# Block-sparse attention followed by a gated feed-forward layer: casting weight loads, g in the norm product, output projection between gate and value products, sums beside AV

## Chip, core and metric

One core of a Trainium2 chip. The metric is the device time of one execution in microseconds (us). Most executions of a kernel lie within 1%; a run counts as slow when it is more than 1.5% above the fastest of its kernel, and comparisons use the others. The profile is one traced execution. Its span is about 2 us shorter than the device time of the same execution, and "time from the start" below means time from the start of that span.

PE is TensorE (matmuls), PEld its weight loads, DVE VectorE, ACT ScalarE, POOL GpSimd, SP the queue that issues plain DMAs.

## The reference

```python
# q, k, v: [4, 8, 768, 64] float32; blocks of 32 tokens, 3 sampled blocks a row of blocks
scores = q @ k.T / 8
mask = |block_i - block_j| <= 1, or either is the first or last block, or block_j is sampled
attn = softmax(where(mask, scores, -1e9))
x = (attn @ v) as [3072, 512]                    # heads side by side
xn = x / sqrt(mean(x*x) + 1e-6) * rms_g
y = (silu(xn @ w_gate) * (xn @ w_val)) @ w_out   # 512 -> 1536 -> 512, float32 out
```

## The kernel before

The work is cut into 8 units of 384 query tokens (2 a batch). Each unit has 4 pairs of heads, and each pair 6 steps. In a step PE makes two score products (128 keys by 384 queries, one for each head) into one of two score tiles (`ps_s`, two PSUM banks each), and ACT takes the exponential of both. Beside it run the attention output (AV), the row sums, the norm, and the feed-forward products of the unit before. The instruction order on every engine is the order in which the program emits it. So the emission order is the schedule, and an instruction that has to wait holds up all that stand behind it on its engine.

The parts that matter here (cuts are marked `# ...`):

```python
# PSUM: 8 banks. ps_s 2 x 2 banks (scores, transposes, norm); ps_a acc, zw; ps_f gp, vp
def load_w_chunk(i):                       # at steps 5, 9, 13, 17
    for w, src, mul in ((wg, wgv, 1.0), (wv, wvv, 0.5)):
        st = wst.tile([P, DM // P, FCH], FP32, name="wstage", tag="wstage")
        # ...
        nc.sync.dma_start(out=st, in_=src[:, :, f0:f0 + FCH])
        for c in range(DM // P):
            nc.vector.tensor_scalar(out=w[:, c, f0:f0 + FCH], in0=st[:, c, :],
                scalar1=gcol[:, c:c + 1], scalar2=mul, op0=ALU.mult, op1=ALU.mult)

def transposes(b, pr):                     # q and k of one pair of heads, 24 products
    t_ = ps_s.tile([P, 2, 1024], BF16, name="tqk", tag="s")
    # ...
    nc.vector.tensor_copy(out=QTe[0:D, sl, :], in_=t_[0:D, 0, 0:S])
    nc.scalar.copy(out=KTe[0:D, sl, :], in_=t_[0:D, 1, 0:S])
    nc.vector.tensor_copy(out=QTo[D:P, sl, :], in_=t_[D:P, 0, 0:S])
    nc.scalar.copy(out=KTo[D:P, sl, :], in_=t_[D:P, 1, 0:S])

def ff_g(u, f):                            # gate: 4 products, tanh on ACT, uu on DVE
    if u == NU - 1:                        # last unit: gate and value in one score tile
        gv = ps_s.tile([P, 2, 512], FP32, name="gv", tag="s"); gp = gv[:, 0, 0:TG]
    else:
        gv = None; gp = ps_f.tile([P, TG], FP32, name="gp", tag="gp")
    # 4 matmuls; th = tanh(gp / 2); uu = (th + 1) * gp

# the schedule: fixed items at a step, feed-forward items by a credit
at(s1 + 1, av, n); at(s1 + 2, zsum, n); at(s1 + 4, wsum, n)
if pr == NP - 1:
    at(s1 + 4, norm_a, u); at(s1 + 5, norm_b, u); at(s1 + 6, norm_c, u)
    at(s1 + 7, norm_d, u, 0); at(s1 + 7, norm_d, u, 1)
# ...
for u in range(NU):
    for f in range(NF):
        items.append((0.64, ff_g, (u, f))); items.append((0.64, ff_v, (u, f)))
    for t in range(NT):                    # output projection after all of them
        for part in range(2):
            items.append((1.3, ff_y, (u, t, part, 2)))
```

The softmax here doesn't subtract the row's maximum and nothing guards it: scores larger than these inputs give would overflow.

Of the kernel before, what the change touches and what calls it, by code (L numbers as in the profile page):

```python
# [17 lines left out]
def kernel(  # L18
# [13 lines left out]
    P = 128  # L32
# [17 lines left out]
    raw = ctx.enter_context(tc.tile_pool(name="raw", bufs=3))  # L50
# [4 lines left out]
    wst = ctx.enter_context(tc.tile_pool(name="wst", bufs=2))  # L55
# [10 lines left out]
    def load_qk(b, pr):  # L66
        qb = raw.tile([P, 2, NC * D], BF16, name="qb", tag="qb")
        kb = raw.tile([P, 2, NC * D], BF16, name="kb", tag="kb")
        nc.gpsimd.dma_start(out=qb, in_=qv[b, :, 2 * pr:2 * pr + 2, :])  # L69
        nc.gpsimd.dma_start(out=kb, in_=kv[b, :, 2 * pr:2 * pr + 2, :])  # L70
        return qb, kb

    vtiles = {}

    def load_v(b, lo, hi):
        if b not in vtiles:
            vtiles[b] = vpool.tile([P, H, NC * D], BF16, name="vb", tag="vb")
        nc.gpsimd.dma_start(out=vtiles[b][:, lo:hi, :], in_=vv[b, :, lo:hi, :])

    qk_raw = {(0, 0): load_qk(0, 0)}  # L80

    ident = const.tile([P, P], BF16, name="ident")
    make_identity(nc, ident)

    samp_i = const.tile([32, NRND], I32, name="samp_i")
# [3 lines left out]
    nc.sync.dma_start(out=samp_i[0:NB, :], in_=s64[:, 0:2 * NRND:2])  # L89
    gcol = const.tile([P, DM // P], FP32, name="gcol")  # L90
    nc.sync.dma_start(out=gcol, in_=moe_rms_g.rearrange("(c p) -> p c", p=P))


    Bm = const.tile([32, 32], BF16, name="Bm")
    nc.gpsimd.memset(Bm, 1.0)
# [11 lines left out]
    jb = const.tile([32, 32], I32, name="jb")  # L107
    nc.gpsimd.iota(jb, pattern=[[1, 32]], base=0, channel_multiplier=0)

    Kind = const.tile([32, NC, P], BF16, name="Kind")  # L110
    nc.gpsimd.memset(Kind, 1.0)
# [6 lines left out]
    Kindf = Kind.rearrange("b c p -> b (c p)")  # L118
    load_v(0, 0, 2)
    for pr in range(1, NP):  # L120
        if pr < 3:
            qk_raw[(0, pr)] = load_qk(0, pr)
        load_v(0, 2 * pr, 2 * pr + 2)
# [4 lines left out]
    nc.vector.tensor_copy(out=samp_f[0:NB, :], in_=samp_i[0:NB, :])  # L128
    onehot = const.tile([32, 32], BF16, name="onehot")
    for r in range(NRND):  # L130
        nc.vector.tensor_scalar(
            out=onehot[0:NB, 0:NB], in0=jbf[0:NB, 0:NB],
            scalar1=samp_f[0:NB, r:r + 1], scalar2=None, op0=ALU.is_equal)
        nc.vector.tensor_tensor(
            out=Bm[0:NB, 0:NB], in0=Bm[0:NB, 0:NB], in1=onehot[0:NB, 0:NB], op=ALU.max)
# [3 lines left out]



    KTe = const.tile([P, NSLOT, S], BF16, name="KTe")
    KTo = const.tile([P, NSLOT, S], BF16, name="KTo")
    QTe = const.tile([P, NSLOT, S], BF16, name="QTe")
    QTo = const.tile([P, NSLOT, S], BF16, name="QTo")
    Qmask = const.tile([32, S], BF16, name="Qmask")
    qm = ps_s.tile([P, 2, 512], FP32, name="qm", tag="s")
    for ic in range(2):
# [3 lines left out]
    nc.vector.tensor_copy(  # L152
        out=Qmask.rearrange("b (i t) -> b i t", i=2), in_=qm[0:32, :, 0:TG])

    def mask_rows(sl):
        for row, KT, QT in ((64, KTe, QTe), (0, KTo, QTo), (32, KTo, QTo)):
            nc.vector.tensor_copy(out=KT[row:row + 32, sl, :], in_=Kindf)
            nc.vector.tensor_copy(out=QT[row:row + 32, sl, :], in_=Qmask)
# [8 lines left out]
    Ew = const.tile([P, NP, 32], BF16, name="Ew")  # L167
    nc.gpsimd.memset(Ew, 0.0)
    for e in range(2):
        h0 = 64 * e  # L170
        nc.gpsimd.affine_select(
            out=Ew[h0:h0 + 64], in_=Ew[h0:h0 + 64], compare_op=ALU.not_equal, fill=1.0,
            base=16 + e, pattern=[[2, NP], [-1, 32]], channel_multiplier=0)
# [3 lines left out]
    for half in range(2):  # L177
# [5 lines left out]
        base=-16, pattern=[[-1, 8]], channel_multiplier=1)  # L183
# [12 lines left out]

    wg = const.tile([P, DM // P, DFF], BF16, name="wg")
    wv = const.tile([P, DM // P, DFF], BF16, name="wv")
    wo = const.tile([P, NF, DM], BF16, name="wo")

    FCH = 384
    wgv = moe_w_gate.rearrange("(c p) f -> p c f", p=P)
    wvv = moe_w_val.rearrange("(c p) f -> p c f", p=P)

    def load_w_chunk(i):
        f0 = i * FCH
        for w, src, mul in ((wg, wgv, 1.0), (wv, wvv, 0.5)):
            st = wst.tile([P, DM // P, FCH], FP32, name="wstage", tag="wstage")
            if i == 0:
                nc.vector.memset(st[0:1, 0, 0:1], 0.0)  # L210
            nc.sync.dma_start(out=st, in_=src[:, :, f0:f0 + FCH])
            for c in range(DM // P):
                nc.vector.tensor_scalar(
                    out=w[:, c, f0:f0 + FCH], in0=st[:, c, :], scalar1=gcol[:, c:c + 1],
                    scalar2=mul, op0=ALU.mult, op1=ALU.mult)

    def load_wo():
        nc.gpsimd.dma_start(out=wo, in_=moe_w_out.rearrange("(c p) f -> p c f", p=P))

    def transposes(b, pr):  # L220
        sl = (b * NP + pr) % NSLOT
        qb, kb = qk_raw.pop((b, pr))
        t_ = ps_s.tile([P, 2, 1024], BF16, name="tqk", tag="s")
        for e, src in enumerate((qb, kb)):
            for c in range(NC):
                for h in range(2):
                    nc.tensor.transpose(  # L227
                        out=t_[64 * h:64 * h + 64, e, c * P:(c + 1) * P],
                        in_=src[:, h, c * D:(c + 1) * D], identity=ident)
        nc.vector.tensor_copy(out=QTe[0:D, sl, :], in_=t_[0:D, 0, 0:S])  # L230
        nc.scalar.copy(out=KTe[0:D, sl, :], in_=t_[0:D, 1, 0:S])  # L231
        nc.vector.tensor_copy(out=QTo[D:P, sl, :], in_=t_[D:P, 0, 0:S])  # L232
        nc.scalar.copy(out=KTo[D:P, sl, :], in_=t_[D:P, 1, 0:S])  # L233
# [3 lines left out]
    def qk_exp(n, jt):  # L237
        u, pr = divmod(n, NP)
        b, ic = divmod(u, 2)
        sl = (b * NP + pr) % NSLOT  # L240
        if jt == 0:
            ptiles[n] = ppool.tile([P, NC, 2, TG], BF16, name="pt", tag="pt")
        s_ = ps_s.tile([P, 2, 512], FP32, name="s_", tag="s")
        for e, (KT, QT, K) in enumerate(((KTe, QTe, 64 + NB), (KTo, QTo, P))):
            nc.tensor.matmul(  # L245
                out=s_[:, e, 0:TG],
                lhsT=KT[0:K, sl, jt * P:(jt + 1) * P],
                rhs=QT[0:K, sl, ic * TG:(ic + 1) * TG], start=True, stop=True)
        nc.scalar.activation(  # L249
            out=ptiles[n][:, jt, :, :], in_=s_[:, :, 0:TG], func=AF.Exp, scale=SCALE)  # L250

    def av(n):
# [3 lines left out]
        if pr == 0:  # L256
            osb[u] = opool.tile([P, NP, TG], FP32, name="osb", tag="osb")
            zwt[u] = ps_a.tile([P, 512], FP32, name="zw", tag="zw")[:, 0:TG]
        o_ = ps_a.tile([P, 512], FP32, name="o_", tag="acc")
        for jt in range(NC):  # L260
            for e in range(2):
                nc.tensor.matmul(  # L262
                    out=o_[64 * e:64 * e + 64, 0:TG],
# [3 lines left out]
        nc.scalar.copy(out=osb[u][:, pr, :], in_=o_[:, 0:TG])  # L267
        o2 = work.tile([P, TG], BF16, name="o2", tag="o2")
        nc.gpsimd.tensor_tensor(
            out=o2, in0=osb[u][:, pr, :], in1=osb[u][:, pr, :], op=ALU.mult)  # L270
        o2s[n] = o2
# [13 lines left out]
    def wsum(n):  # L285
        u, pr = divmod(n, NP)
        nc.tensor.matmul(
            out=zwt[u][0:32, :], lhsT=Ew[:, pr, :], rhs=o2s.pop(n),
            start=False, stop=(pr == NP - 1), skip_group_check=True)

    nrm = {}

    def norm_a(u):
        zs = work.tile([P, TG], FP32, name="zs", tag="zs")
        nc.vector.tensor_copy(out=zs, in_=zwt.pop(u))
        nrm[u] = zs

    def norm_b(u):
        zs = nrm[u]
        zt = ps_s.tile([P, NT, 16], FP32, name="zt", tag="s")  # L300
        for t in range(NT):
            nc.tensor.matmul(
                out=zt[:, t, :], lhsT=zs[:, t * P:(t + 1) * P], rhs=Sel,
                start=True, stop=True)
        rz = work.tile([P, NT, 8], FP32, name="rz", tag="rz")
        nc.vector.reciprocal(out=rz, in_=zt[:, :, 0:8])
        w1 = work.tile([P, NT, 8], FP32, name="w1", tag="w1")
        nc.vector.tensor_tensor(out=w1, in0=zt[:, :, 8:16], in1=rz, op=ALU.mult)
# [6 lines left out]
        nc.gpsimd.tensor_tensor(out=rs, in0=ms, in1=nhalf, op=ALU.pow)  # L315
        fx = work.tile([P, NT, 8], FP32, name="fx", tag="fx")
# [7 lines left out]
    def norm_c(u):  # L324
# [10 lines left out]
    def norm_d(u, half):  # L335
# [4 lines left out]
        for i in range(2):  # L340
# [4 lines left out]
        nc.vector.tensor_tensor(  # L345
            out=xns[u][:, 2 * half:2 * half + 2, :],
            in0=osb[u][:, 2 * half:2 * half + 2, :], in1=fb[:, :, 0:TG], op=ALU.mult)
# [3 lines left out]
    def ff_g(u, f):  # L351
        if f == 0:
            hps[u] = ffw.tile([P, NF, TG], BF16, name="hp", tag="hp", bufs=2)
        if u == NU - 1:
            gv = ps_s.tile([P, 2, 512], FP32, name="gv", tag="s")
            gp = gv[:, 0, 0:TG]
        else:
            gv = None
            gp = ps_f.tile([P, TG], FP32, name="gp", tag="gp")
# [9 lines left out]
        gst[(u, f)] = (uu, gv)  # L369

    def ff_v(u, f):
# [133 lines left out]
```

## Time and profile before

The median is 485.74 us (485.72 to 487.21, 3 runs). The profiled execution took 489.61 us, with a span of 487.7 us.

| stretch of the profiled run | us |
|---|---|
| first exponential starts | 16.5 |
| 36th exponential starts (end of "the opening") | 87.3 |
| 36th to last exponential | 337.8 |
| last exponential to the end | 62.6 |
| 24 steps (one unit) in the middle, mean of five | 53.2 |
| PE idle before an instruction, after the 36th exponential, summed | 57.8 |

From the page: busy time of the engines, then the span in 40 slices. A digit is a busy share in tenths (9 is 90% or more). PEclk is the granted PE clock in tenths of full speed.

```profile
span 487.7 us, 6743 instructions
...
PE 385.8 (79%) x2730; PEld 189.7 (39%) x2730; DVE 185.6 (38%) x392; ACT 251.4 (52%) x385; POOL 73.0 (15%) x112
...
PE   1554387988788978998788989997889989987556
...
PEclk9985787999899999999899999999998999998999
```

PE is busiest, but its row has low digits at the start (up to the seventh slice) and at the end, and 7s in between. The PEclk row has many digits below 9. (Its first two digits say little: the record of the granted clock begins with its first change, 27.2 us from the start, and the score products before that last 0.51 us, as they do at half clock, against 0.33 us at full clock.)

The opening, from the timeline (start, duration, engine, line, operation, then in brackets the idle time of that engine just before it and what ended it):

```profile
29.40 0.50 PE L227 MATMUL tqk<-ident,kb 128*64 128x128 bf16 x12
...
36.95 1.41 DVE L213 TENSOR_SCALAR wv<-wstage,gcol 128x384 bf16<-128x384 f32 x4 [6.15 <-DMA wstage<-in_moe_w_val_dram]
...
40.30 0.55 DVE L230 COPY QTe<-tqk 64x768 bf16<-64x768 bf16 x1
...
42.30 0.79 ACT L233 COPY KTo<-tqk 64x768 bf16<-64x768 bf16 x1 [0.63 <-DVE QTo L232]
...
43.15 0.48 PE L245 MATMUL s__421<-QTe,KTe 88*128 88x384 bf16 x1 [12.38 <-ACT KTo L233]
```

The transposes of the third pair end at 29.9 us. Their first copy on DVE starts at 40.30 us, because DVE first stands at the weight scaling of `wv` until the staged load has landed (6.15 us of idle), and then makes six mask copies (38.39 to 40.27 us). The transposes hold one of the two score tiles until their last copy ends, on ACT at 43.1 us, and the exponential that would free the other stands behind that copy on ACT. So the next score product (`s__421`) waits 12.38 us on PE.

What PE waited for in the whole run, from the view of waits (who, for whom: us in total, times, longest):

```profile
PE gp L361 <- DVE uu L367: 18.9, 35, 2.0
PE gv L375 <- DVE uu L367: 14.0, 12, 1.2
PE s__421 L245 <- ACT KTo L233: 12.4, 1, 12.4
...
PE s__526 L245 <- ACT KTo L233: 7.2, 1, 7.2
PE ft L328 <- DVE FHL_192 L321: 6.7, 4, 2.5
PE ft L328 <- DVE FHL_193 L321: 4.0, 3, 1.5
```

The gate bank is single. One round of it in the timeline of all engines:

```profile
297.72 0.81 PE L361 MATMUL gp<-xn,wg 128*128 128x384 bf16 x4 [0.40 <-DVE uu L367]
...
298.57 0.49 ACT L365 ACTIVATE th<-gp 128x384 bf16<-128x384 f32 x1 [0.40 <-PE gp L361]
...
299.09 0.55 DVE L367 SCALAR_TENSOR_TENSOR uu<-th,gp 128x384 bf16<-128x384 bf16 x1 [0.76 <-ACT th L365]
...
299.70 0.81 PE L361 MATMUL gp<-xn,wg 128*128 128x384 bf16 x4 [0.18 <-DVE uu L367]
```

Gate product to next gate product is 1.98 us: product, tanh, uu, next product. The value products and a step's score products do not fill it, and PE waits 0.18 to 0.40 us here.

Last, the clock, from busy times by stretch (PE, PEld, DVE, ACT, POOL busy with counts, then granted clock, DMA share, GB/s):

```profile
350.00:351.00 1.00, 0.00 (x0) 0.00 (x0) 0.36 (x1) 1.00 (x3) 0.00 (x0) 1.00 0.00 0
...
352.00:353.00 1.00, 1.00 (x5) 0.47 (x4) 0.00 (x0) 0.35 (x1) 0.00 (x0) 0.50 0.00 0
```

After a gap of about 1.3 us and others just before it, the granted clock is 0.50 for 3.4 us. Adding up the record after the 36th exponential gives 20.5 us at half clock.

### The profile page before, as it was taken

The page shows a single profiled execution, that of the slowest core. Times are in us where ns is not written, and L with a number is a line of the kernel's source. Part 1 is how long each engine was busy: PE and PEld are TensorE (multiplying, and loading weights), DVE is VectorE, ACT ScalarE, POOL GpSimd, SP SyncE. Part 2 cuts the span into 40 slices and gives each one's busy share as a digit, 9 for nine tenths or more (in the row PEclk, how much of TensorE's full clock was granted, in tenths as well). Part 3 has the DMA queues.
Part 4 walks back from the last instruction along what each step waited for, and adds up shares of the span by engine and source line. Part 5 has one row for each costly group of instructions (what it writes and reads, how often), then busy time and mean ns, then how long its engine had stood idle before and what let it go on. Part 6 is the DMA issues. An engine that isn't in the chain of part 4 may idle for free.

```text
span 487.7 us, 6743 instructions
## 1 busy us (share of the span) xinstructions
PE 385.8 (79%) x2730; PEld 189.7 (39%) x2730; DVE 185.6 (38%) x392; ACT 251.4 (52%) x385; POOL 73.0 (15%) x112
## 2 busy tenths in 40 slices
PE   1554387988788978998788989997889989987556
PEld 1221133444344434544344434543344434433322
DVE  4416743542344412443244333434244224433440
ACT  1534474665466644675466646665556546612121
POOL 8710122011011011011111020010000010010000
PEclk9985787999899999999899999999998999998999
DMA  5976762311322013223032015021000000010001
GB/s 68 146 186 215 195 102 42 53 24 31 77 34 32 2 43 53 35 34 55 30 46 34 0 44 87 1 34 43 23 1 0 23 30 15 0 40 27 1 0 65
DMA packets 22786, 24.02 MB, mean 49 GB/s; under 512 B 1764, under 2 KB 19684, under 8 KB 22756
## 3 DMA queue, kind: packets, MB, share of 16 engines
q0 software_dynamic: 14464, 11.01, 16.2%
q1 hardware_dynamic: 8292, 12.59, 7.3%
q8 instruction: 21, 0.34, 0.3%
q14 instruction: 9, 0.07, 0.1%
HBM read 28.31 MB, written 6.29 MB: 71 GB/s over the span
## 4 chain that ended last, share of the span: by engine, by line
PE 57%; DVE 15%; ACT 15%; issue 5%; DMA 4%; POOL 2%; POOLq 0%; ACTq 0%; DVEq 0%
PE gp L361 11%; PE yp L389 11%; PE vp L375 7%; DVE uu L367 5%; ACT th L365 5%; PE zw L280 4%; ACT pt L249 3%; ACT KTe L231 3%; DMA wstage<-in_moe_w_val_dram 3%; PE tqk L227 2%; PE gv L375 2%; ACT KTo L233 2%; DVE QTo L232 2%; DVE QTe L230 2%; PE gv L361 2%
## 5 line engine op out<-in xcount | busy, mean ns | idle before, releaser
L367 DVE SCALAR_TENSOR_TENSOR uu<-th,gp 128x384 bf16<-128x384 bf16 x84 | 46.5, 554 | 104.0 <-ACT th L365 104.0
L361 PE MATMUL gp<-xn,wg 128*128 128x384 bf16 x336 | 70.0, 331 | 18.9 <-DVE uu L367 18.9
L389 PE MATMUL yp<-wo,hp 128*128 128x512 bf16 x288 | 73.7, 398 | 6.1 <-ACT yo L395 3.4
L375 PE MATMUL vp<-xn,wv 128*128 128x384 bf16 x336 | 69.9, 331 | 1.3 <-DVE hp L378 1.3
L365 ACT ACTIVATE th<-gp 128x384 bf16<-128x384 f32 x84 | 41.2, 490 | 35.9 <-PE gp L361 35.1
L378 DVE TENSOR_TENSOR hp<-uu,vp 128x384 bf16<-128x384 bf16 x84 | 46.6, 554 | 25.5 <-PE vp L375 19.0
L361 PEld LDWEIGHTS <-wg 128*128 128x128 bf16 x384 | 35.4, 98 | 53.4 <-issue 34.4
L375 PEld LDWEIGHTS <-wv 128*128 128x128 bf16 x384 | 35.6, 98 | 46.9 <-issue 26.5
L389 PEld LDWEIGHTS <-hp 128*128 128x128 bf16 x288 | 28.3, 103 | 39.5 <-issue 15.1
L245 PEld LDWEIGHTS <-KTo 128*128 128x128 bf16 x192 | 19.4, 101 | 42.8 <-issue 30.8
L395 ACT COPY yo<-yp 128x512 f32<-128x512 f32 x24 | 14.0, 585 | 34.5 <-PE yp L389 34.3
L231 ACT COPY KTe<-tqk 64x768 bf16<-64x768 bf16 x16 | 12.7, 792 | 36.2 <-DVE QTe L230 36.2
L245 PEld LDWEIGHTS <-KTe 88*128 88x128 bf16 x192 | 19.6, 102 | 26.3 <-issue 10.3
L262 PEld LDWEIGHTS <-vb 128*64 128x64 bf16 x384 | 21.0, 117 | 21.4 <-issue 13.7
L280 PE MATMUL zw<-pt,Ez 128*32 128x384 bf16 x384 | 22.2, 338 | 0.0
L230 DVE COPY QTe<-tqk 64x768 bf16<-64x768 bf16 x16 | 8.8, 550 | 33.2 <-PE tqk L227 33.0
L345 DVE TENSOR_TENSOR xn<-osb,fb 128x768 bf16<-128x768 f32 x16 | 14.8, 952 | 16.7 <-PE fb L342 16.6
L375 PE MATMUL gv<-xn,wv 128*128 128x384 bf16 x48 | 9.7, 324 | 14.0 <-DVE uu L367 14.0
L365 ACT ACTIVATE th<-gv 128x384 bf16<-128x384 f32 x12 | 5.9, 490 | 23.6 <-PE gv L361 23.5
L233 ACT COPY KTo<-tqk 64x768 bf16<-64x768 bf16 x16 | 12.7, 793 | 10.0 <-DVE QTo L232 10.0
L69 POOL DMA_DIRECT2D qb<-in_q_dram x16 | 12.3, 768 | 25.9 <-PE tqk L227 25.1
L315 POOL TENSOR_TENSOR rs<-ms,nhalf 128x3 f32<-128x3 f32 x8 | 7.0, 869 | 51.5 <-DVE ms L312 51.5
(800 smaller groups left out, 568.6 us busy)
## 6 DMA issues: line engine op xcount, KB each, us to landing
out_dram<-yo SPq DMA_DIRECT2D x24, 256.0 KB, 2.0
qb<-in_q_dram POOLq DMA_DIRECT2D x16, 192.0 KB, 3.8
kb<-in_k_dram POOLq DMA_DIRECT2D x16, 192.0 KB, 4.3
wstage<-in_moe_w_gate_dram SPq DMA_DIRECT2D x4, 768.0 KB, 6.4
wstage<-in_moe_w_val_dram SPq DMA_DIRECT2D x4, 768.0 KB, 5.9
vb<-in_v_dram POOLq DMA_DIRECT2D x3, 768.0 KB, 7.2
wo<-in_moe_w_out_dram POOLq DMA_DIRECT2D x1, 1536.0 KB, 11.9
vb<-in_v_dram POOLq DMA_DIRECT2D x4, 192.0 KB, 6.2
```

The lines of the kernel that those rows point to most:

```text
L230: nc.vector.tensor_copy(out=QTe[0:D, sl, :], in_=t_[0:D, 0, 0:S])
L231: nc.scalar.copy(out=KTe[0:D, sl, :], in_=t_[0:D, 1, 0:S])
L233: nc.scalar.copy(out=KTo[D:P, sl, :], in_=t_[D:P, 1, 0:S])
L245: nc.tensor.matmul(out=s_[:, e, 0:TG], lhsT=KT[0:K, sl, jt * P:(jt + 1) * P], rhs=QT[0:K, sl, ic * TG:(ic + 1) * TG], start=True, stop=True)
L262: nc.tensor.matmul(out=o_[64 * e:64 * e + 64, 0:TG], lhsT=vb[:, 2 * pr + e, jt * D:(jt + 1) * D], rhs=pt_[:, jt, e, :], start=(jt == 0), s ...
L280: nc.tensor.matmul(out=zwt[u][32 * c:32 * c + 32, :], lhsT=Ez[:, pr, :], rhs=pt_[:, 2 * j2 + par, e, :], start=(pr == 0 and j2 == 0), stop ...
L361: nc.tensor.matmul(out=gp, lhsT=wg[:, c, f * P:(f + 1) * P], rhs=xns[u][:, c, :], start=(c == 0), stop=(c == NP - 1))
L365: nc.scalar.activation(out=th, in_=gp, func=AF.Tanh, scale=0.5)
L367: nc.vector.scalar_tensor_tensor(out=uu, in0=th, scalar=1.0, in1=gp, op0=ALU.add, op1=ALU.mult)
L375: nc.tensor.matmul(out=vp, lhsT=wv[:, c, f * P:(f + 1) * P], rhs=xns[u][:, c, :], start=(c == 0), stop=(c == NP - 1))
L378: nc.vector.tensor_tensor(out=hps[u][:, f, :], in0=uu, in1=vp, op=ALU.mult)
L389: nc.tensor.matmul(out=yp, lhsT=hps[u][:, f, t * P:(t + 1) * P], rhs=wo[:, f, :], start=(f == 0), stop=(f == NF - 1))
```

## The change

The intent is to keep PE supplied throughout. The weights come in bf16 by casting loads, so DVE no longer scales them; g goes into the norm product and the factor 0.5 into the output copy. The output projection of the unit before is spread between the gate and value products of this one. The row sums come straight after AV, and the square sums of a unit come together at its end, as a set of four products in four column groups of PE, in place of four single products at four times. Further parts belong to it: transposes are evicted by two DVE copies in place of four alternating ones, osb and most output copies move from ACT to DVE, AV uses a score bank from pair 8 on, norm steps are spread over more steps, the last unit's gate and value products alternate between two kinds of bank, and q and k are loaded by whole batches.

```diff
-    def load_w_chunk(i):  ... staged float32 loads, 8 DVE scalings a chunk ...
+    def load_w(i):
+        nc.gpsimd.dma_start(out=wg[:, :, i * FH:(i + 1) * FH], in_=wgv[:, :, ...])
+        nc.gpsimd.dma_start(out=wv[:, :, i * FH:(i + 1) * FH], in_=wvv[:, :, ...])
@@ norm product @@
-        nc.vector.tensor_tensor(out=xns[u][:, 2 * half:2 * half + 2, :], in0=osb..., in1=fb..., op=ALU.mult)
+        for i in range(2):
+            nc.vector.scalar_tensor_tensor(out=xns[u][:, pr, :], in0=osb[u][:, pr, :],
+                scalar=gcol[:, pr:pr + 1], in1=fb[:, i, 0:TG], op0=ALU.mult, op1=ALU.mult)
@@ transposes @@
-        four copies QTe (DVE), KTe (ACT), QTo (DVE), KTo (ACT)
+        nc.vector.tensor_copy(out=XE[0:D, sl], in_=t_[0:D, :, 0:S])
+        nc.vector.tensor_copy(out=XO[D:P, sl], in_=t_[D:P, :, 0:S])
@@ mask rows: all slots before the first step @@
+    load_w(0); mask_rows(2); load_w(1); mask_rows(3); load_wo(); mask_rows(4); mask_rows(5)
@@ schedule @@
-        at(s1 + 1, av, n); at(s1 + 2, zsum, n); at(s1 + 4, wsum, n)
+        at(s1 + 1, 1.1, av, n, n >= 8); at(s1 + 1, 0.7, zsum, n)
-            norm_a .. norm_d at s1 + 4, + 5, + 6, + 7, + 7
+            norm_a .. norm_e at s1 + 4, + 5, + 7, + 8, + 9, + 10
@@ feed-forward queue @@
-    gate and value of unit u, then 6 projection parts of unit u
+    for f in range(NF):
+        ffq.append((avail, 0.65, ff_g, (u, f, wide)))
+        ffq.append((avail, 0.65, ff_v, (u, f, wide)))
+        ffq.append((avail, 0.65, ff_y, (u - 1, f // 4, f % 4, 4)))
```

(The loops that guard the first and last unit, and the set-up of constants, are left out.)

## The prediction

> **What bounds the kernel now.** The page gives PE 79% busy of a 487.7 us span, ACT 52%, DVE 38%: PE is the bound, but only in the middle. From the starts of exponentials and tanh in the timeline:
>
> - Opening: the 36th exponential starts at 87.3 us. DVE's in-order weight scaling waits for staged weights (6.6 and 6.2 us) ahead of the copies of the transposes: the score product waits 12.4 us, then 7.2 us (waits view, 22 to 60 us).
> - Middle: 52.4 us a unit of 24 steps. Start-to-start times of dense matmuls (0.162 us for 384 columns, 0.216 for 512, about 1.7 us for AV plus sums, 0.7 for a set of transposes) add up to some 43 us; 9 are idle: at the single gate bank (gate, tanh 0.49, uu 0.55, next gate: 1.98 us cycle), at the norm chain (1.5 us before ft, 8 times) and at the transposes' four serial copies (2.9 us, holding a score bank).
> - Tail: last exponential at 425.1 us, then 62.6 us. The last unit's gate/value pairs take 2.63 us each for 1.3 us of products; its output projection comes after.
>
> **What changes.**
> 1. Casting weight loads, g in the norm product: removes 32 scalings (11.9 us of DVE) and, more, their waits. The Trainium skill, "DMA: Bandwidth & Descriptors", section "SWDGE vs HWDGE vs iDMA", says a casting DMA must be issued from GpSimd; in this trace that queue moved 11.01 MB for 16.2% of 16 engines' span, some 139 GB/s flat out. By that estimate 7 MB of first inputs and weights needs about 51 us, in the order of need; no stall expected.
> 2. New cost: the mask copies of all other slots (20 x about 0.35 us) stand ahead of the second transposes' copies on DVE: a 6 to 9 us hole after the first three exponentials. First exponential at about 13 us instead of 16.5, 36th at about 60 instead of 87: 27 us won.
> 3. Output projection between gate and value: successive gate products lie about 2.3 us of PE work apart, over the 1.98 us cycle. Norm steps are spread. Transposes: two DVE copies of about 1 us; they still hold a score bank, and I expect 1.9 us lost, 12 times, less than before.
> 4. ACT gives osb, most yo and KT copies to DVE; estimate 26 us a unit on each, neither bounding.
>
> **Sum.** From step 35 on, dense PE work is about 309 us; transposes' holds 23; first unit without projection 5; norms and rest 11; output 4. 60 + 352 = 412 us span, less 2 (span against time here): **410 us**, range 392 to 432. Faster by over 2%: 0.97; within 2%: 0.02; slower: 0.01.
>
> **What would show it.** Right: no PE wait for DMA at 30 to 60 us; the middle at about 46 us a unit; PE above 88% busy from 80 us on; tanh of the last unit about 2.0 us apart; the largest remaining PE wait is the score product behind DVE copies XE/XO. Wrong: gate products still waiting for uu; wo or wg awaited.
>
> **What would make it wrong.** The clock: the Trainium skill, "TensorE: Matmul & The Clock Gate", section "What's actually happening", says an idle window halves the PE clock until it has been busy for about 3.4 us. This trace agrees: after idle at 350 and 364 us the granted clock is 0.50. If 1.9 us holds trigger it, add up to 20 us; if not, the gain is larger, since before pays it. Other risks: GpSimd slowed by issuing weight loads, delaying mask rows; DVE queue order delaying uu.

## The result, and the profile after

The changed kernel takes 402.1 us median (399.99 to 406.36, 4 runs) against 486.48 us (485.72 to 488.08, 4 runs). The ratio is 0.8247, with a 95% interval of 0.8186 to 0.8309. Ratios are the mean time of one kernel's fast runs over that of the other's of the same rounds, so they are not quite the ratio of the medians. In these four runs the granted clock was 1.0 twice (399.99 and 400.38 us) and 0.977 to 0.979 twice (403.82 and 406.36 us, the latter counted as slow). The profiled executions are one of 489.61 us before and the fastest, of 399.99 us, after, so the differences of the stretches below add up to some 5 us more than those of the medians.

The same lines of the page:

```profile
span 398.3 us, 6628 instructions
...
PE 352.3 (88%) x2730; PEld 187.0 (47%) x2730; DVE 217.8 (55%) x423; ACT 200.4 (50%) x301; POOL 66.8 (17%) x95
...
PE   2657879887799999998999999998999999999986
...
PEclk9999999999999999999999999999999999999999
```

From the twelfth slice on PE is at 9 nearly everywhere, and the clock row has 9 throughout. For the first 27.3 us that 9 is no measurement: here too the record begins only then, and the score products before it last 0.51 us, against 0.33 us afterwards.

| stretch | before | after | difference |
|---|---|---|---|
| first exponential starts | 16.5 | 11.7 | -4.8 |
| 36th exponential starts | 87.3 | 59.0 | -28.3 |
| from there to the end | 400.3 | 339.3 | -61.0 |
| of that, PE idle before an instruction | 57.8 | 19.4 | -38.4 |
| of that, time at half clock | 20.5 | 0.0 | -20.5 |
| recorded time at half clock in the opening | 30.7 | 0.0 | -30.7 |
| one unit in the middle, mean of five | 53.2 | 42.9 | -10.3 |
| last exponential to the end | 62.6 | 58.9 | -3.7 |

(The last line holds more work than before: at the last exponential 9 of the 12 gate and value steps of the seventh unit are still to come.)

The waits of PE after the change, in the same view:

```profile
PE tqk L161 <- DMA qb<-in_q_dram: 5.1, 1, 5.1
...
PE ft L327 <- ACT pt L242: 2.7, 3, 0.9
...
PE gp L361 <- DVE uu L367: 2.4, 9, 0.5
...
PE s__283 L238 <- ACT pt L242: 0.9, 1, 0.9
```

The gate product's wait for uu has fallen from 18.9 to 2.4 us, and the last unit's (`gv`, 14.0 us) is gone. A round of the gate in the middle shows why:

```profile
240.17 0.81 PE L361 MATMUL gp<-xn,wg 128*128 128x384 bf16 x4
...
240.82 0.81 PE L378 MATMUL vp<-xn,wv 128*128 128x384 bf16 x4
241.07 0.48 ACT L365 ACTIVATE th<-gp 128x384 bf16<-128x384 f32 x1
...
241.59 0.55 DVE L367 SCALAR_TENSOR_TENSOR uu<-th,gp 128x384 bf16<-128x384 bf16 x1 [0.86 <-ACT th L365]
...
241.80 0.81 PE L392 MATMUL yp<-wo,hp 128*128 128x512 bf16 x3
...
242.44 0.81 PE L361 MATMUL gp<-xn,wg 128*128 128x384 bf16 x4
```

The chain of gate, tanh and uu ends at 242.14 us, but PE has value, score and projection products to do until 242.44 us. The next gate product starts with no wait. What is left is seen after each set of transposes (PE alone):

```profile
248.83 0.50 PE L161 MATMUL tqk<-ident,kb 128*64 128x128 bf16 x12
...
249.44 0.33 PE L238 MATMUL s__2944<-XO 128*128 128x384 bf16 x1
250.66 0.32 PE L238 MATMUL s__2948<-XE 88*128 88x384 bf16 x1 [0.90 <-ACT pt L242]
```

The product at 250.66 us waits 0.90 us for an exponential. Such a wait stands after each of the twelve sets of transposes in the rest, nine times before a score product and three times before `ft`. The transposes hold one score bank, so the next two steps share the other.

### The profile page after: what moved, and what is told of

The parts are those of the page before. It is cut to its first block, busy times and chain, and to the rows that moved or that the text cites. A ratio compares the mean times of both kernels' runs of the same rounds, so it can differ in the third digit from the quotient of the medians.

```text
span 398.3 us, 6628 instructions
## 1 busy us (share of the span) xinstructions
PE 352.3 (88%) x2730; PEld 187.0 (47%) x2730; DVE 217.8 (55%) x423; ACT 200.4 (50%) x301; POOL 66.8 (17%) x95
## 4 chain that ended last, share of the span: by engine, by line
PE 79%; ACT 9%; DVE 8%; issue 2%; DMA 1%; POOL 1%; DVEq 0%; POOLq 0%; ACTq 0%
PE gp L361 14%; PE yp L392 14%; PE vp L378 13%; ACT pt L242 6%; PE zw L275 5%; PE tqk L161 3%; PE oa L259 2%; DVE uu L367 2%; ACT th L365 1%; PE fb L341 1%; PE zt L295 1%; DVE xn L346 1%; DMA out_dram<-yo 1%; PE gw L361 1%; DVE XE L183 1%
## 5 line engine op out<-in xcount | busy, mean ns | idle before, releaser
L238 PEld LDWEIGHTS <-XO 128*128 128x128 bf16 x192 | 19.0, 99 | 40.7 <-issue 30.8
L238 PEld LDWEIGHTS <-XE 88*128 88x128 bf16 x192 | 19.1, 99 | 26.5 <-issue 6.7
L259 PEld LDWEIGHTS <-vb 128*64 128x64 bf16 x384 | 19.5, 111 | 17.7 <-issue 11.1
L346 DVE SCALAR_TENSOR_TENSOR xn<-osb,gcol,fb 128x384 bf16<-128x384 f32 x32 | 18.2, 610 | 9.0 <-PE fb L341 9.0
L164 DVE COPY XE<-tqk 64x1536 bf16<-64x1536 bf16 x16 | 15.2, 949 | 11.5 <-PE tqk L161 11.5
L165 DVE COPY XO<-tqk 64x1536 bf16<-64x1536 bf16 x16 | 15.4, 960 | 0.2
L401 DVE TENSOR_SCALAR yo<-yp 128x512 f32<-128x512 f32 x21 | 14.4, 685 | 1.2 <-PE yp L392 1.1
L161 PE MATMUL tqk<-ident,qb 128*64 128x128 bf16 x192 | 9.1, 234 | 5.3 <-DMA qb<-in_q_dram 5.1
L264 DVE COPY osb<-oa 128x384 f32<-128x384 f32 x8 | 4.5, 556 | 17.1 <-PE oa L259 17.1
L275 PEld LDWEIGHTS <-Ez 128*32 128x32 bf16 x384 | 7.3, 95 | 11.8 <-issue 10.1
L161 PEld LDWEIGHTS <-qb 128*64 128x64 bf16 x192 | 6.4, 116 | 10.4 <-issue 5.3
## 6 DMA issues: line engine op xcount, KB each, us to landing
kb<-in_k_dram POOLq DMA_DIRECT2D x3, 768.0 KB, 10.3
```

What stands on the lines that cost most here:

```text
L161: nc.tensor.transpose(out=t_[64 * h:64 * h + 64, e, c * P:(c + 1) * P], in_=src[:, 2 * pr + h, c * D:(c + 1) * D], identity=ident)
L238: nc.tensor.matmul(out=s_[:, e, 0:TG], lhsT=X[0:K, sl, 1, jt * P:(jt + 1) * P], rhs=X[0:K, sl, 0, ic * TG:(ic + 1) * TG], start=True, stop ...
L259: nc.tensor.matmul(out=o_[64 * e:64 * e + 64, :], lhsT=vb[:, 2 * pr + e, jt * D:(jt + 1) * D], rhs=pt_[:, jt, e, :], start=(jt == 0), stop ...
L275: nc.tensor.matmul(out=zwt[u][32 * c:32 * c + 32, :], lhsT=Ez[:, pr, :], rhs=pt_[:, 2 * j2 + par, e, :], start=(pr == 0 and j2 == 0), stop ...
L346: nc.vector.scalar_tensor_tensor(out=xns[u][:, pr, :], in0=osb[u][:, pr, :], scalar=gcol[:, pr:pr + 1], in1=fb[:, i, 0:TG], op0=ALU.mult, ...
```

## The experiments

All were correct within the tolerance. "Opening" is the start of the 36th exponential in the profiled run, "rest" is from there to the end of the span. The rest of the changed kernel was 339.3 us in both profiles of it. Its opening was 59.0 and 61.4 us.

| run | edit | median us | ratio to before | opening | rest | PE idle in the rest | half clock, opening / rest |
|---|---|---|---|---|---|---|---|
| before | | 488.17 to 489.43 | 1 | 87.3 | 400.3 | 57.8 | 30.7 / 20.5 |
| r_after | the change again | 404.18 | 0.8251 (0.8214 to 0.8288) | 61.4 | 339.3 | 21.0 | 3.4 / 0.0 |
| b1_cast | before + casting loads | 473.73 | 0.9692 (0.9663 to 0.9721) | 70.5 | 402.8 | 57.6 | 10.2 / 27.3 |
| e2_stage | change - casting loads | 418.14 | 0.8567 (0.8525 to 0.8610) | 77.2 | 339.2 | 19.4 | 30.7 / 0.0 |
| e1_seq | change - interleaving | 427.36 | 0.8756 (0.8709 to 0.8803) | 60.3 | 364.7 | 36.0 | 3.4 / 0.0 |
| e7_act | change, osb and yo on ACT | 402.47 | 0.8244 (0.8203 to 0.8285) | 60.8 | 340.5 | 19.0 | 13.7 / 3.4 |
| e6_sums | change - sums beside AV | 399.75 | 0.8179 (0.8155 to 0.8203) | 57.6 | 340.9 | 14.0 | 10.2 / 3.4 |
| e8_norm | change - spread norm | 427.55 | 0.8733 (0.8705 to 0.8760) | 64.2 | 361.7 | 37.0 | 10.2 / 13.7 |
| e9_copies | change, four alternating copies | 447.53 | 0.9157 (0.9131 to 0.9182) | 74.4 | 371.7 | 39.1 | 10.2 / 34.1 |
| e10_last | change, last unit in one tile | 421.22 | 0.8587 (0.8556 to 0.8618) | 63.0 | 356.3 | 34.6 | 6.8 / 3.4 |
| e3_masks | change + late mask copies | 399.64 | 0.8164 (0.8127 to 0.8201) | 55.8 | 340.8 | 21.0 | 3.4 / 3.4 |
| e4_fill | change + filled steps | 398.93 | 0.8163 (0.8129 to 0.8197) | 64.3 | 334.9 | 14.2 | 14.5 / 6.0 |
| e11_best | both + row sums a step later | 387.01 | 0.7914 (0.7892 to 0.7936) | 53.7 | 331.3 | 13.9 | 3.4 / 0.0 |

(The last column is us at half clock in the profiled run: in the opening as far as recorded, in the rest up to PE's last product.) b1, e1, e2 and e7 ran on one chip in one set; r_after, e3, e4 and e6 in a second; e8, e9, e10 and e11 in a third, each set with its own runs of before. The changed kernel itself was run again only in the second set, so across sets the ratios are compared, not the times.

The opening also differs where no edit touches it: e10_last changes only the last unit, and its opening was 63.0 us, against 59.0 and 61.4 us. The recorded half clock in it differs too (6.8, 0.0 and 3.4 us). So differences of a few us in the opening are not put down to an edit on their own.

The theory: two separate gains. In the opening, DVE no longer waits for staged weights ahead of the copies that PE needs. In the rest, PE is the bound, and the change closes its waits, above all that of the gate bank, by putting other products there. The rivals are named in each expectation.

### b1_cast: the kernel before with casting loads alone

```diff
-            nc.sync.dma_start(out=st, in_=src[:, :, f0:f0 + FCH])   # and 4 DVE scalings
+            nc.gpsimd.dma_start(out=w[:, :, f0:f0 + FCH], in_=src[:, :, f0:f0 + FCH])
@@ g in the norm product, yo = 0.5 * yp on ACT @@
```

> The kernel before with only the weight loads changed: casting loads on the GpSimd queue, g in the norm product, 0.5 in the output copy. Theory A (the opening was held by the weight scaling standing in DVE's order and waiting for the staged loads): the 36th exponential starts at about 62 to 70 us instead of 87.3, the 12.4 us and 7.2 us waits of the score product are gone, time 460 to 470 us. Rival B (the opening is held by the arrival of q, k, v or by score banks, and other parts of the change won it): 36th exponential after 80 us, time 478 us or more. Middle and tail as before, 52 us a unit, in both.

The time was 473.73 us. The 12.4 and 7.2 us waits were gone. The 36th exponential came at 70.5 us, 16.8 us earlier, just outside the span that I had given, and the time missed it by 4 us. So the weight staging is the largest part of the opening's 28.3 us, but not all of it. The rest did not gain (402.8 us; 27.3 us of it at half clock, against 20.5).

### e2_stage: the change with staged loads again

```diff
+            nc.sync.dma_start(out=st, in_=src[:, :, f0:f0 + FCH])   # fp32 stage, steps 5, 9, 13, 17
+            for c in range(DM // P):
+                nc.vector.tensor_copy(out=w[:, c, f0:f0 + FCH], in_=st[:, c, :])
```

> The changed kernel with the weights staged as float32 through the SP queue and copied to bf16 by DVE in the places of the old scaling (no g, so the result stays right). Theory A: DVE's copies wait for the staged loads ahead of the transposes' copies; the 36th exponential goes from 59 to 72 to 85 us and the time to 413 to 428 us. Rival B: 36th exponential before 64 us, time 406 us or less.

The time was 418.14 us, the 36th exponential came at 77.2 us, and the rest was 339.2 us, that of the changed kernel to a tenth. Taking the staging out of one kernel gave 16.8 us, and putting it into the other cost 15.8 to 18.2 us. Part of this may be the clock: with staging both openings have 30.7 us at recorded half clock, without it 10.2 (b1_cast) and 0.0 or 3.4 us (the changed kernel). What the waits alone would cost was not separated. Two waits of the score product behind DVE's copies were back, in the view of waits:

```profile
PE s__403 L243 <- DVE XE L171: 8.0, 1, 8.0
PE s__309 L243 <- DVE XE L171: 7.6, 1, 7.6
```

Rival B falls. What the weights do not explain of the opening (some 10 to 12 us) belongs to other parts: the first exponential is 4.8 us earlier (in b1_cast it is still at 16.5 us), and the remainder was not tried part by part.

### e1_seq: projection after the gate and value products

```diff
         for f in range(NF):
             ffq.append((avail, 0.65, ff_g, (u, f, wide)))
             ffq.append((avail, 0.65, ff_v, (u, f, wide)))
-            ffq.append((avail, 0.65, ff_y, (u - 1, f // 4, f % 4, 4)))
+        for f in range(NF):
+            ffq.append((avail, 0.65, ff_y, (u, f // 4, f % 4, 4)))
```

> The changed kernel with the output projection put back after all gate and value products of its unit, nothing else changed. Theory A (the projection between gate and value gives PE the work that covers the 1.98 us gate cycle): gate products wait again for uu, about 0.35 us at some 80 of them, the middle goes from 42.9 to about 46 to 47 us a unit, and the last unit loses little as its gates have two banks; time 422 to 440 us. Rival C (the middle was sped up by the score-bank AV, the moved evictions and the spread norm steps; the order of the products is of no account): 408 us or less.

The time was 427.36 us, a unit in the middle took 47.4 us, and the rest grew by 25.4 us. The waits of PE (whole run) were the one named, and one that I had not named: projection products in a row wait for the eviction of their single bank.

```profile
PE gp L361 <- DVE uu L367: 12.8, 48, 0.9
PE yp L392 <- DVE yo L401: 8.1, 12, 1.2
```

Rival C falls. The waits add up to 21 us. The idle times of PE in the rest grew by only 16.6 us, for a cost of 25.4. A matmul's end is modelled late in the profile (0.33 us for one that is followed after 0.162 us when the stream is dense), so by estimate each wait costs some 0.165 us more than its idle time says. There are 92 waits in the rest here against 38 in the changed kernel, and 54 times 0.165 us is 8.9 us. That would close the sum; it was not tested in another way.

### e7_act: osb and yo back on ACT

```diff
-        nc.vector.tensor_copy(out=osb[u][:, pr, :], in_=o_)
+        nc.scalar.copy(out=osb[u][:, pr, :], in_=o_)
@@ and yo: nc.scalar.activation(out=yo, in_=yp, func=AF.Copy, scale=0.5) for every unit @@
```

> The changed kernel with the copies of osb and yo given back to ACT. Theory A (ACT, 50% busy, bounds nothing in the middle): 400 to 408 us, tanh and exponentials start at most a few tenths of a microsecond later. Rival D (the evictions leaving ACT are what made PE dense): 415 us or more, with score products waiting for exponentials.

The time was 402.47 us, no difference beyond noise (ratio 0.8244, against 0.8247 and 0.8251 for the changed kernel), and the rest was 340.5 us. Rival D falls: which engine copies these does not matter here.

### r_after, e3_masks, e4_fill, e6_sums

> The changed kernel itself, as the yardstick of these runs: 400 to 404 us, some executions at a granted clock near 0.98 and up to 406 us.

404.18 us, clock between 0.969 and 1.0 in its six runs; the fastest run had clock 1.0 (400.38 us), the slowest 0.969 (407.93 us).

e3_masks moves the DVE mask copies of slots 1 to 5 behind the transposes' copies:

```diff
-    mask_rows(1) ... mask_rows(5)                 # all before step 0
+    zero_rows(1) ... zero_rows(5)                 # only POOL's zero rows stay there
+    for sl, step in ((1, 1), (2, 7), (3, 13), (4, 20), (5, 22)):
+        at(step, 0, mask_rows, sl)
```

> The changed kernel with the mask copies of slots 1 to 5 put behind the transposes' copies of their slot in DVE's order. Theory A (the prediction's hole: those 20 copies hold the second transposes' copies): the seventh exponential starts at about 18 us instead of 24.8, score products 3 to 5 no longer come 1.7 us apart, and 4 to 7 us of it reach the end: 394 to 398 us. Rival E (the opening is then held by the arrival of q, k and v, or by ACT): the seventh exponential may come earlier but the 36th stays within 2 us of 59, time within 2 us of the changed kernel.

The time was 399.64 us, about 1.1% below r_after by the ratios. The seventh exponential came at 19.3 us instead of 24.8 or 25.1, the 36th at 55.8. In the changed kernel exponentials 3 to 6 were 1.7 us apart and then came a hole (ACT alone, from the timeline):

```profile
16.50 0.81 ACT L242 ACTIVATE pt<-s__283 128x768 bf16<-128x768 f32 x1 [0.88 <-PE s__283 L238]
18.20 0.81 ACT L242 ACTIVATE pt<-s__287 128x768 bf16<-128x768 f32 x1 [0.89 <-PE s__287 L238]
19.89 0.81 ACT L242 ACTIVATE pt<-s__291 128x768 bf16<-128x768 f32 x1 [0.88 <-PE s__291 L238]
24.75 0.81 ACT L242 ACTIVATE pt<-s__296 128x768 bf16<-128x768 f32 x1 [4.05 <-PE s__296 L238]
```

With the copies late, the same stretch (exponentials 4 to 7) takes 2.4 us:

```profile
16.87 0.81 ACT L244 ACTIVATE pt<-s__267 128x768 bf16<-128x768 f32 x1 [0.88 <-PE s__267 L240]
17.57 0.80 ACT L244 ACTIVATE pt<-s__271 128x768 bf16<-128x768 f32 x1
18.57 0.81 ACT L244 ACTIVATE pt<-s__275 128x768 bf16<-128x768 f32 x1 [0.19 <-PE s__275 L240]
19.27 0.81 ACT L244 ACTIVATE pt<-s__280 128x768 bf16<-128x768 f32 x1
```

So the hole is real, and its cause is the one in the prediction. Of the 5.5 us at the seventh exponential, 3 to 6 us are left at the 36th; against r_after, with the same 3.4 us of recorded half clock in the opening, it is 5.6 us. In the medians of all runs 4.5 us are left, in the lower part of what theory A gave. The time of 399.64 us was above the 394 to 398 us that I had written, because r_after itself ran 2 us slower than I had assumed.

e4_fill books the cost of the transposes two steps later, so the credit puts feed-forward products into the step after them:

```diff
-        at(6 * (8 * b + pr) - 5, 0.8, transposes, b, pr)
+        at(6 * (8 * b + pr) - 5, 0, transposes, b, pr)
+        at(6 * (8 * b + pr) - 3, 0.8, lambda: None)
```

> The changed kernel with the 0.8 us that the schedule books for a set of transposes booked two steps later, so that gate, value or projection products stand between the two score products after it. Theory A (the transposes hold a score bank; PE then waits about 0.9 us for one exponential, 12 times, and nothing else holds it there): these waits shrink to about 0.2 us, time 6 to 11 us less, 391 to 396 us. Rival F (ACT or DVE is late there too, so the wait only moves to the next gate or score product): within 3 us of the changed kernel.

The time was 398.93 us and the rest 334.9 us, 4.4 us less. PE idle in the rest fell by 5 to 7 us; the score products' part of it fell from 11.1 to 4.8. Less than the 6 to 11 us of theory A, more than rival F. This profile had 6.0 us at half clock in the rest, which the changed kernel's profiles did not have, so part of the saving may have been given back there.

e6_sums has the sums as in the kernel before:

```diff
-        at(s1 + 1, 0.7, zsum, n)
+        at(s1 + 2, 0.7, zsum, n)
+        at(s1 + 4, 0.35, wsum, n)                 # one square-sum product a pair, all in rows 0 to 31
@@ norm_a: without the four products in four column groups @@
```

> The changed kernel with the sums as before: row sums one step after AV, one square-sum product a pair (32 of them) instead of eight sets of four. From the trace one such product takes about 0.42 us of PE (0.165 and the 0.256 us before it), 32 make 13.5 us, against about 0.4 us for each set of four, 3 us; the row sums' own change of weights adds some 0.1 us, 32 times. Theory A (PE is the bound, every removed product counts): 8 to 14 us more, 408 to 416 us. Rival G (these products fit in PE's idle times): within 4 us of the changed kernel.

The time was 399.75 us, 0.9% below r_after by the ratios, where theory A said 8 to 14 us more. The theory failed for this part. The trace shows one reason: with the row sums one step later, the step after the transposes holds row sums instead of nothing, so most of the 0.9 us waits are gone (score products' idle in the rest 3.7 us instead of 11.1). The extra square-sum products are there (32 singles, 0.27 us from the start of one to the next product, where dense products follow after 0.162 us): PE's busy time in the rest is 7.1 us longer than in the changed kernel's first profile (with 3.4 us at half clock in it), its idle time 5.4 us shorter. The two halves of "sums beside AV" pull against each other. I did not run them singly, so their single sizes stay open.

### e8_norm, e9_copies, e10_last: other parts undone

e8_norm puts the norm steps as close together as before:

```diff
-            at(s1 + 7, 0.0, norm_c, u); at(s1 + 8, 0.3, norm_d, u)
-            at(s1 + 9, 0.35, norm_e, u, 0); at(s1 + 10, 0.35, norm_e, u, 1)
+            at(s1 + 5, 0.0, norm_c, u); at(s1 + 6, 0.3, norm_d, u)
+            at(s1 + 7, 0.35, norm_e, u, 0); at(s1 + 7, 0.35, norm_e, u, 1)
```

> The changed kernel with the norm steps as close together as before (scale chain in the step of its transposing product, ft one step later, both halves of xn in the next). Theory A: the chain from zt to fh (about 3 us with the 0.87 us power on GpSimd) no longer fits in the 1.65 us of one step, ft waits 1 to 1.6 us eight times as in the kernel before, and from the 36th exponential to the end it takes 8 to 14 us more than the 339 us of the changed kernel: 408 to 416 us. Rival: the interleaved products cover it, 405 us or less.

427.55 us, and the rest 22.4 us longer, more than the 8 to 14 us expected. The waits for ft were there, and longer than I had said (view of waits):

```profile
PE ft L327 <- DVE FHL L320: 16.4, 8, 2.3
```

Each is 1.6 to 2.3 us. After four of the seven in the rest the clock is at half for 3.4 us, 13.7 us in all; after the other three (1.60, 1.61 and 2.25 us) it stays full.

e9_copies has the four alternating copies again:

```diff
-        nc.vector.tensor_copy(out=XE[0:D, sl], in_=t_[0:D, :, 0:S])
-        nc.vector.tensor_copy(out=XO[D:P, sl], in_=t_[D:P, :, 0:S])
+        DVE XE q, ACT XE k, DVE XO q, ACT XO k, each 64x768
```

> The changed kernel with the transposes evicted as before, in four copies that alternate between DVE and ACT one after the other. Theory A: the score bank is held some 2.9 us and the exponential of the next step stands behind the copies on ACT, so PE waits about 2.5 us instead of 0.9, twelve times; from the 36th exponential to the end 12 to 25 us more than 339 us, and some halved clock after the waits; 412 to 428 us. Rival: this eviction is off the path, 405 us or less.

447.53 us. The twelve waits were 2.46 us each, as expected, but the cost was higher: 32.4 us in the rest and 13 to 15 us in the opening. In the opening, ACT's copies wait for DVE's, which stand behind the mask copies, and the exponentials stand behind ACT's copies; one score product waits 13.4 us. In the rest there are nine stretches at half clock, 34.1 us in all, around these waits; one is shown here. First the wait, from the timeline, then the stretches around it, in the columns used for the clock above:

```profile
289.65 0.79 ACT L167 COPY XO<-tqk 64x768 bf16<-64x768 bf16 x1 [0.63 <-DVE XO L166]
...
290.50 0.32 PE L240 MATMUL s__2974<-XE 88*128 88x384 bf16 x1 [2.46 <-ACT XO L167]
```

```profile
287.50:290.50 3.00, 0.54 (x7) 0.22 (x4) 1.11 (x2) 1.62 (x3) 0.22 (x1) 1.00 0.02 5
...
292.00:294.00 2.00, 2.00 (x8) 0.99 (x7) 0.00 (x0) 0.48 (x1) 0.00 (x0) 0.50 0.00 0
```

The kernel before has these same four copies and hardly paid for them: score products idle 3.0 us in its whole rest, and its trace shows why: its transposes stand three steps ahead of their pair's first product, and other products follow them (at 346 us from the start: a score step, a square sum, four gate and four value products, and only then the next score product, which waits 0.47 us). This is read from the trace and was not tested by a run of the old order in the new kernel. I had counted them as one of its costs, and that was wrong.

e10_last puts the last unit's gate and value products into two halves of one tile:

```diff
-        if wide:
-            gp = ps_s.tile([P, 2, 512], FP32, name="gw", tag="s")[:, 0, 0:TG]
+        if u == NU - 1:
+            gv = ps_s.tile([P, 2, 512], FP32, name="gv", tag="s"); gp = gv[:, 0, 0:TG]
@@ value: gv[:, 1, 0:TG] @@
```

> The changed kernel with gate and value products of the last unit in two halves of one score tile, as before, instead of in turn in two kinds of bank. Theory A: the value products wait for uu again, 1.17 us each, twelve times, though the projection of the unit before stands between: 10 to 15 us more, all of it after the last exponential: 411 to 417 us. Rival: with the projection interleaved the tail is covered, 405 us or less.

421.22 us; the tail grew from 58.9 to 74.4 us, the rest by 17.0, of which up to 1.7 us may be the clock (3.4 us at half, an estimate). The waits are those of the kernel before, 12 times 1.17 us, and the interleaved projection does not cover them, since the value product itself waits and holds all that is behind it:

```profile
PE gv L380 <- DVE uu L369: 14.0, 12, 1.2
```

### e11_best

```diff
 e3_masks and e4_fill together, and
-        at(s1 + 1, 0.7, zsum, n)
+        at(s1 + 2, 0.7, zsum, n)                  # square sums stay in eight sets of four
```

> Late mask copies and filled steps after the transposes together, with the row sums one step after AV (which the sums run showed to fill the same steps) and the square sums in eight sets of four as in the changed kernel. The two single changes gave 4.3 us each; if they add (theory A: PE is the bound and each removed wait counts), 391 to 396 us; if they share one cause (rival), 397 to 400 us.

387.01 us (386.72 to 388.55), ratio 0.7914, interval 0.7892 to 0.7936: faster than expected, and 4.1% below the changed kernel by the ratios. The opening was 53.7 us, the rest 331.3 us. Its page shows the row of PE at 9 nearly everywhere from the eleventh slice on, and no digit of the clock below 9 (3.4 us at half clock, in the opening, are spread over two slices):

```profile
span 385.0 us, 6601 instructions
...
PE   2678889997999999997999999998999999999985
...
PEclk9999999999999999999999999999999999999999
```

The two single changes gave about 1.1% each. The third edit, the row sums, was run alone only together with the costlier square sums (e6_sums), so its own share is not separated. Its runs also stayed at a clock of 0.986 or more, while those of e3 and e4 went down to 0.973.

## Why the prediction was right or wrong, point by point

- **The time.** 410 us (392 to 432) was predicted and 402.1 measured. The direction, the size and the two main mechanisms hold. One step of the sum was wrong: an execution takes 1.7 to 1.9 us more than its span (489.61 against 487.7, 399.99 against 398.3), so a span of 412 us means about 414. "Less 2" set the span of one slower execution of the kernel before against the median of others.
- **Opening, "27 us won".** Measured 28.3 us (87.3 to 59.0). The staged weights carry 16 to 18 us of it (b1_cast, e2_stage), waits and the half clock that came with them together. First exponential: 13 predicted, 11.7 measured.
- **"A 6 to 9 us hole after the first three exponentials."** The cause was right (e3_masks: 5.5 us earlier at the seventh exponential). Its form was not: I had taken the two score banks to be given out strictly in turn. In fact steps 3 to 6 went on through the one free bank, 1.7 us apart, and the hole came after the sixth.
- **"No stall expected" from the loads.** Right. After the opening the profile shows no PE wait for a DMA; the only one above 1 us is for the first q (5.1 us). The last weights land about 45 us from the start, against the estimate of 51.
- **"Successive gate products lie about 2.3 us of PE work apart, over the 1.98 us cycle."** Right: 2.27 us in the round shown, the gate's wait fell from 18.9 to 2.4 us, and undoing it costs 25.4 us (e1_seq, which also brings 8.1 us of waits for the projection's bank).
- **"Transposes' holds 23", 1.9 us lost 12 times.** This is the term that was mis-sized. Measured are twelve waits of 0.90 us, 10.8 us (nine before a score product, three before `ft`); all idle of score products in the rest is 11.1 us. The reason is the same bank again: the second score product after the transposes gets the other bank when its exponential is done, before the copies are. The sum was to be 352 us from step 35 on, and 339.3 was measured; 12 of the 13 us between them are this term. (The other terms add up to 329 us, and 339.3 less 10.8 is 328.5. They were not checked singly.) "Less than before" was wrong in sign: score products idled 3.0 us in the rest of the kernel before. The change made these holes by leaving the step after the transposes without other work, and e4_fill and e11_best show that they can be filled.
- **"The middle at about 46 us a unit"**: 42.9. The smaller holes give some 2 of the 3 us (12 us over six and a half units); the remainder is open.
- **"PE above 88% busy from 80 us on"**: 297.2 of 318 us, 93%. **Tanh of the last unit "about 2.0 us apart"**: 1.95.
- **"The largest remaining PE wait is the score product behind DVE copies XE/XO."** Half right. The largest group is the score product beside the transposes (11.1 us), but what ends its wait is the exponential.
- **The clock.** Named as a risk, it became a gain: no wait in the rest of the changed kernel is over 1.13 us, and its half clock time is 0, against 20.5 us before. At half clock, gate products follow each other after 0.320 us, at full clock after 0.162 us, so dense work takes twice as long, and up to about 10 us of the 61 (an estimate) come from that. The opening has another 30.7 us of recorded half clock before and none after, which by the same estimate is at most 15 of its 28.3 us, and less in truth, since PE also waited there. Some waits are followed by half clock, so part of what removing a wait won came through the clock.
- **"Neither bounding" of ACT and DVE.** Right as far as e7_act shows: moving the copies of osb and yo between them changed nothing.
- **Square sums: "8 sets of 4".** The effect was not shown. e6_sums was not slower, and its two parts offset each other.

How the 61 us of the rest divide can't be read from the runs that undo one part. Interleaving (25.4), spread norm (22.4), two copies (32.4) and the last unit's banks (17.0) add to 97 us, so a part undone in the dense kernel costs more than it can have cost in the old one, in e8_norm and e9_copies with half clock on top (13.7 and 34.1 us). The profile of before gives another division: of the 38.4 us less PE idle, 16.2 is the gate bank, 14.0 the last unit, 5 each the norm's ft and the projection's bank, and the transposes cost 8.1 more; smaller waits make up the remaining 6. The other 22.6 us are less PE busy time: half clock (up to 10 us by the estimate above), the late ends of waits (85 before, 38 after: 47 times 0.165 us, 7.8 us by estimate) and fewer square-sum products; their shares were not separated. AV in a score bank and the loads of q and k by whole batches were not undone in any run, so their share is not known.

## What to carry to other kernels

On an in-order engine that is the bound, look at each chain that goes out to another engine and comes back (here gate, tanh, uu: 1.98 us), and place at least that much independent work between its two ends; then check that a new order has not emptied the steps that used to hide another wait. Take work that waits for a slow load out of the queue that feeds the bound, even if it is itself cheap. When a part is undone for a test, its cost is that in the new kernel, and such costs do not add. Read the record of the clock beside each stretch, and check from the length of products where that record begins.

## What the Trainium skill lacked or had wrong

- "TensorE: Matmul & The Clock Gate", section "What's actually happening", gives an idle window of about 3.4 us as what halves the clock. Here shorter waits did it: 2.46 us in e9_copies (granted clock 0.50 afterwards, 34.1 us at half clock in the rest), 2.1 to 2.3 us in e8_norm (13.7 us), and in the kernel before a wait of 1.32 us shortly after one of 0.47 us. (A later section of the page has frequent short idles between groups of matmuls make the clock go to and fro, without a length.) The length of a wait alone does not decide it: one of 2.25 us in e8_norm was not followed by half clock, and single waits of up to 1.13 us in the changed kernel were not (0.0 us). The time that the page gives for getting back to full clock, about 3.4 us busy, agrees: stretches at half clock last 3.4 us or a multiple of it.
- "Trainium Kernel Development and Optimization", section "Performance Expectations", says that matmul busy time is a bad metric for how close a kernel is to roofline, because matmuls are pipelined. It gives no size for what this hides of a wait. In e1_seq the idle times of the rest grew by 16.6 us and the rest by 25.4 us, which fits 0.165 us hidden in each of 54 more waits (an estimate).
- "DMA: Bandwidth & Descriptors", section "SWDGE vs HWDGE vs iDMA", says where a casting load must be issued; no page gives its rate. In the changed kernel the first inputs and all weights, 7.1 MB as bf16, had landed 44.6 us from the start, and slices in which the DMA row is at 9 moved 172 to 205 GB/s. My estimate of 139 GB/s from shares of packet time was too low.
- No page has what an engine's wait costs when the program order leaves nothing behind it: with the same four copies of the transposes the score products idle 3.0 us in the rest of the kernel before, and 24.3 us in that of the changed kernel (e9_copies).
